# A retention layer and two MLPs on one core: the order of GpSimd's key scaling, of the weight decoding and of the last activations in the opening

## The chip, the cores and the metric

The kernel runs on one core of a Trainium2 chip. The metric is the device time of one execution in microseconds (us). A run here is one execution; the time given is the median of three.

## The reference, cut to what matters

q, k and v have 8 batches, 8 heads, 576 positions and 64 columns per head. All arithmetic is in float32. Retention is causal attention without softmax: each score is multiplied by a power of the head's decay.

```python
scores = (1 / sqrt(64)) * q @ k.T
ret = (scores * Dmat) @ v            # Dmat = gamma**(i-j) where i >= j, else 0
x = ret, heads side by side          # 4608 tokens x 512
h = x @ moe_w_in                     # 512 -> 2048
x2 = (h * sigmoid(1.702 * h)) @ moe_w_out
h2 = x2 @ moe2_w_in
out = (h2 - tanh(h2)) @ moe2_w_out   # 4608 x 512
```

## The kernel before, in words

The 4608 tokens are 36 tiles of 128 tokens; four tiles make a block of 512 tokens, and there are 9 blocks. Retention runs in chunks of 64 tokens with a carried state per head (`s_at`), so that a tile needs four groups of small products on TensorE (the PE of the profile): its scores (line 314), the carried part from the state (line 285), the scores times v (line 368, "values"), and the new state from k and v (line 338, "states"). Ahead of these the decay is put into the operands: `at_scale(t)` multiplies the keys that go into the states by a table (line 262, always on GpSimd, the profile's POOL) and the queries by another (line 263, on VectorE, the profile's DVE, for tiles 0 to 3, and on GpSimd for later tiles). The states of tile t need the keys of tile t and the first half of tile t+1.

`x_out` adds the two parts of a tile's result (lines 386, 391, 393, on DVE) and splits it into a high and a low fp32r half, `xh` (line 396, ScalarE, the profile's ACT) and `xl` (line 399, DVE). Each large product is three passes over four chunks of 128 rows (high by high, high by low, low by high), so 12 matmuls of 128x512: `mm_in` (line 527) for a first-MLP product h of one of 16 column groups f with one block, into a PSUM bank. `act_a` then runs tanh on ACT (line 540) and one DVE instruction (line 542) that reads the bank and so frees it.

The weights come as int64 words that hold float64 numbers, and are decoded on the chip. A chunk of weights takes three pieces, and `dec_piece` issues the next one, in this order per chunk: the load of a chunk ahead and `dec_b` of the chunk before (DVE line 134, ACT line 148); `dec_d` of the chunk before (DVE line 155) and `dec_a` of this one (ACT line 118, DVE line 122); `dec_a2` (DVE line 127). Chunk f, up to 15, yields `win[f]`, the operand of product f; it is complete when piece 3f+4 has run `dec_d`.

Each engine runs its instructions in the order in which the program lists them; that order is written out by hand at the end of the kernel function. The opening has these parts:

- **First visits** (`first_visit`, t = -1 to 3): the retention of tiles 0 to 3. Ahead of visit t stands `at_scale(t + 1)`; inside it, `dec_piece(pieces)` stands just ahead of `x_out`, and `follow(t)` issues the load of tile t+4 (from ACT's queue) and its scaling on GpSimd. Tile 4 takes the buffer of tile 0. Visit 3 ends with the first large product.
- **f loop** (f = 0 to 3): product f, two pieces, the activations, a visit (tiles 4 to 7), one piece, and what is left of the visit (`visit_out`: xl and the new state).
- **k loop** (k = 0 to 11): products 4+k of block 0 and the 16 products of block 1, with three pieces for each k and four from k = 8, and the visits of tiles 8 to 11 at k = 1, 4, 7 and 10. `activate(2)` leaves two products without their activation. The 32 products of the opening are numbered n = 0 to 31; even n take one of two banks `ps_h`, odd n one of two banks `acc` in turn, but for n = 31.
- **End of the opening**: the carried products of tile 12, the last two activations, and then the main loop over s from 32, whose first `mm_in` takes a bank of `ps_h`.

After that come the rest of retention, both MLPs, and the decoding and rearranging of the second MLP's weights.

Of the kernel before, what the change touches and what calls it, by code (L numbers as in the profile page):

```python
# [15 lines left out]
ALU = mybir.AluOpType  # L16

P = 128
HEADS = 8
HD = 64  # L20
# [7 lines left out]
NF = DFF // P  # L28
HP = HEADS // 2
TILES = NT // P  # L30
TPB = BLK // P
# [18 lines left out]
def kernel(  # L50
# [11 lines left out]
    nc = tc.nc  # L62
# [18 lines left out]
    qt_sb = tabs.tile([P, KD, P], F32, name="qt_sb")  # L81
    mt_sb = tabs.tile([P, 2, HP, HD], F32, name="mt_sb")
    mk_sb = tabs.tile([P, 1, HD], F32, name="mk_sb")
    jt_sb = tabs.tile([P, HEADS, 1], F32, name="jt_sb")
# [46 lines left out]
    def dec_b(m, f, c):  # L131
        _, z = half.pop((m, f, c))
        lo = stg.pop((m, f, c)).bitcast(U32).rearrange("p (n two) -> p n two", two=2)[:, :, 0]
        nc.vector.scalar_tensor_tensor(
            out=z, in0=lo, scalar=29, in1=z, op0=ALU.logical_shift_right, op1=ALU.bitwise_or
        )
        o = z.bitcast(F32)
        if (m, c) == (1, 0):
            part[m, f, c] = o
            return  # L140
        if (m, c) == (0, 0):
            s = win[f] = wts.tile([P, 2, KD, P], F32R, tag=f"wi{f}", name="wi")
            sv = s.rearrange("p a k c -> p a (k c)")
        elif m == 0 and f % 5 < 3:
            sv = wos_p.tile([P, 2, DM], F32R, tag="wos", name="ws")
        else:
            sv = st_p.tile([P, 2, DM], F32R, tag="ws", name="ws", bufs=2)
        nc.scalar.activation(out=sv[:, 0], in_=o, func=ACTF.Copy)
        half[m, f, c] = o, sv

    def dec_d(m, f, c):
        if (m, c) == (1, 0):
            return
        o, sv = half.pop((m, f, c))
        nc.vector.tensor_tensor(out=sv[:, 1], in0=o, in1=sv[:, 0].bitcast(F32), op=ALU.subtract)
        if (m, c) != (0, 0):
            part[m, f, c] = sv
        if (m, c) == (0, 1):
            wos[f] = sv

    def dec_store():
        while part:
            (m, f, c), sv = part.popitem()
            if (m, c) == (1, 0):
                w2_d[f] = dram.tile([P, BLK], F32, tag=f"w{m}{f}{c}", name="wr")
                nc.sync.dma_start(out=w2_d[f], in_=sv)
                continue
            d = dram.tile([P, 2 * DM], F32, tag=f"w{m}{f}{c}", name="wd")
            nc.sync.dma_start(out=d, in_=sv.rearrange("p a n -> p (a n)").bitcast(F32))
            wo_d[m, f] = d  # L170
# [6 lines left out]
    def dec_load(n):  # L177
        while n_load[0] < min(n, len(chunks)):
            wload(*chunks[n_load[0]])
            n_load[0] += 1  # L180

    def dec_piece(pieces=1):

        for _ in range(pieces):
            n, k = divmod(n_dec[0], 3)
            if k == 2:
                dec_store()
            if n > len(chunks):
                return
            n_dec[0] += 1  # L190
            if k == 0:
                dec_load(n + 2)
                if n:
                    dec_b(*chunks[n - 1])
                continue
            if k == 1 and n:
                dec_d(*chunks[n - 1])
            if n < len(chunks):
                (dec_a if k == 1 else dec_a2)(*chunks[n])
# [50 lines left out]
            (nc.scalar if TPB <= t < START + 2 else nc.sync).dma_start(out=a, in_=attn[t])  # L250
        at[t] = parts

    def at_scale(t):
        if t >= TILES:
            return
        for hp in (slice(0, 2), slice(2, HP)) if t == 0 else (slice(0, HP),):
            n = hp.stop - hp.start
            qv, kv = (
                at[t][i][:, 0, hp.start * P:hp.stop * P].rearrange("p (h d) -> p h d", d=d) for i, d in enumerate((P, HD))
            )  # L260
            j = jt_sb[:, 2 * hp.start:2 * hp.stop].to_broadcast([P, 2 * n, HD])
            nc.gpsimd.tensor_tensor(out=kv, in0=kv, in1=j, op=ALU.mult)
            (nc.gpsimd if t >= TPB else nc.vector).tensor_tensor(out=qv, in0=qv, in1=qt_sb[:, hp], op=ALU.mult)

    pat = ps_a.tile([P, 2, BLK], F32, name="pat")
    def halves(i):
        return slice(i * HD, (i + 1) * HD)

    def pos(t, c):
        return (2 * t + c) % CHUNKS  # L270

    def token(c):
        return slice(c * HD, (c + 1) * HD)
# [4 lines left out]
    def tile_carried(t, banks):  # L278

        parts = [c for c in (1, 0) if pos(t, c)]  # L280
        inner = [bank[:, high].rearrange("p (a c) -> p a c", a=2) for bank in banks]
        for c in parts:
            for hp in range(HP):
                for i in range(2):
                    nc.tensor.matmul(  # L285
                        inner[hp % 2][halves(i ^ hp % 2), hp // 2, token(c)], lhsT=s_at[c][halves(i), hp],
                        rhs=at[t][0][halves(i), 0, hp * P:(hp + 1) * P][:, token(c)],
                        start=True, stop=True, skip_group_check=True,
                    )
# [131 lines left out]
    def acc_pair(i):  # L421
        return [ps_acc.tile([P, BLK], F32, tag=f"acc{2 * i + b}", name="sc") for b in range(2)]

    def first_visit(t, pieces):

        banks = acc_pair(t % 2)
        last = t == TPB - 1
        if not last:
            tile_scores(t + 1, banks)
        if t < 0:  # L430
            new, parts = tile_states(t)
            scores_out(t + 1, banks)
            for _ in states_out(t, new, parts):
                pass
            return
        tile_values(t)
        new, parts = tile_states(t)
        tile_carried(t, banks)
        out = states_out(t, new, parts)
        next(out)  # L440
        if not last:
            scores_out(t + 1, banks)
        next(out)
        carried_out(t, banks)
        dec_piece(pieces)
        low_out = x_out(t)
        follow(t)
        low_out()
        if last:
            product(0)  # L450
            tile_scores(t + 1, banks)
            scores_out(t + 1, banks)

    def follow(t):
        for u in {8: (10,), 9: (11,), 10: (12,), 11: (13,)}.get(t, (t + 4,) if t < 6 else ()):
            at_load(u)
            at_scale(u)
# [3 lines left out]
    def visit_out():  # L461
        while later:
            later.pop(0)()
# [49 lines left out]

    def mm_in(s, n=None):
        j, f = divmod(s, NF)
        if n is not None and n % 2 and n < 2 * NF - 2:
            h = ps_acc.tile([P, BLK], F32, tag=f"acc{n // 2 % 2}", name="h")
        elif acc_free and s % 2 and s > PAUSE:
            h = ps_acc.tile([P, BLK], F32, tag=f"acc{acc_free.pop(0)}", name="h")
        else:  # L520
            h = ps_h.tile([P, BLK], F32, tag="h", name="h")
        hps[s] = h
        xs = (xh[j], xl[j])
        n = 0
        for k in range(KD):
            for a, b in PASS:
                nc.tensor.matmul(  # L527
                    h, lhsT=win[f][:, a, k], rhs=xs[b][:, k], start=(n == 0), stop=(n == 3 * KD - 1)
                )
                n += 1  # L530
# [36 lines left out]
    def g_store(s):  # L567
        gd[s] = dram.tile([P, BLK], F32, tag=f"g{s}", name="gd")
        nc.sync.dma_start(out=gd[s], in_=tt.pop(s))
# [277 lines left out]
    for c in range(2):  # L847
        r = halves(c)
        j = jt_sb[r].rearrange("p (h i) o -> p i h o", i=2)
        for b in range(2):  # L850
            nc.vector.tensor_tensor(
                out=mt_sb[r, b], in0=mk_sb[r].to_broadcast([HD, HP, HD]), in1=j[:, b ^ c].to_broadcast([HD, HP, HD]),
                op=ALU.mult,
# [7 lines left out]
    def product(s):  # L861
        mm_in(s, next(order))
        queue.append(s)

    def activate(keep):
        while len(queue) > keep:
            s = queue.pop(0)
            act_a(s, next(n_a))
            kept.append(s)
            if len(kept) > 2:  # L870
                g_store(kept.pop(0))

    def visit():
        attn_visit("all", False)
        follow(seen["rest"])

    for t in range(-1, TPB):
        if t + 1 < TPB:
            at_scale(t + 1)
        first_visit(t, t)  # L880

    for f in range(TPB):
        if f:
# [7 lines left out]
    for k in range(NF - TPB):  # L891
        product(TPB + k)
        activate(2)
        dec_piece()
        product(next(n_one))
        activate(2)
        dec_piece()
        if k % 3 == 0:
            product(next(n_one))
            activate(2)  # L900
        if k % 3 == 1:
            visit()
        dec_piece(2 if k > 7 else 1)
        visit_out()
    tile_carried(START, both)
    activate(0)
    carried_out(START, both)
    while kept:
        g_store(kept.pop(0))
# [17 lines left out]
    for s in range(LAG, NB * NF):  # L927
        j, f = divmod(s, NF)
# [73 lines left out]
    for u in range(pairs * QS):  # L1002
# [17 lines left out]
        n = 4 if final else 3  # L1020
# [122 lines left out]
```

## Time and profile before

| | |
|---|---|
| median of 3 runs | 1692.25 us (1690.43 to 1694.17) |
| profiled execution: its time | 1690.12 us |
| its span, first to last instruction | 1688.3 us |
| mean granted TensorE clock over the span | 0.981 |
| PE busy | 1626.7 us, 96% of the span |
| DVE busy | 1071.1 us, 63% |
| ACT busy | 866.8 us, 51% |
| POOL busy | 115.4 us, 7% |

Time lost shows as TensorE's idle time, some 62 us, and as time in which its granted clock is 0.5, which is 1.2 GHz, in place of 1.0, which is 2.4 GHz. Starts in the rows below are counted from the start of the span.

### The profile page before, as it was taken

Reading aid. Unit: us, or ns where it says so; the run is one execution under the profiler, and the core shown is the slowest. Engines: PE = TensorE matmul, PEld = TensorE weight load, DVE = VectorE, ACT = ScalarE, POOL = GpSimd, SP = SyncE. Lnnn points to the kernel's source line nnn. Section 1 sums busy time; section 2 is a strip of 40 time slices with the busy share of each in tenths; the row PEclk is TensorE's granted clock in tenths of the full one; section 3 lists DMA queues with packets and bytes.
Section 4 is the critical chain, followed back from the end, with each engine's and each line's share of the span. In section 5 each row is a group of like instructions: output and inputs, shape, how many; then the busy total and the mean of one; then the engine's idle time right before and its main releaser. Section 6 shows DMA issues by size and latency. Waiting matters only on the chain.

```text
span 1688.3 us, 29158 instructions
## 1 busy us (share of the span) xinstructions
PE 1626.7 (96%) x11082; PEld 1339.4 (79%) x11082; DVE 1071.1 (63%) x1664; ACT 866.8 (51%) x1602; POOL 115.4 (7%) x106
## 2 busy tenths in 40 slices
PE   3599899999999999999999999999999999999999
PEld 2477688888888888888888888888888888888887
DVE  2576676656666553566667786777767776667532
ACT  1344444334444443455556666666656666656532
POOL 1211111122123300000000000000000000000000
PEclk5799999999999999999999999999999999999999
DMA  6455666888889846897999889898998898989962
GB/s 195 151 178 193 205 225 226 272 293 300 294 310 345 290 163 216 285 344 272 336 348 317 288 320 341 317 338 275 326 351 316 315 318 301 310 302 320 360 214 87
DMA packets 166300, 470.96 MB, mean 279 GB/s; under 512 B 18576, under 2 KB 27792, under 8 KB 156944
## 3 DMA queue, kind: packets, MB, share of 16 engines
q1 hardware_dynamic: 153904, 439.68, 74.8%
q10 hardware_dynamic: 12256, 29.40, 4.9%
q8 instruction: 88, 1.44, 0.4%
q14 instruction: 52, 0.43, 0.1%
HBM read 349.48 MB, written 119.54 MB: 278 GB/s over the span
## 4 chain that ended last, share of the span: by engine, by line
PE 93%; DVE 2%; DMA 2%; ACT 1%; issue 1%; POOL 0%; ACTq 0%; POOLq 0%; DVEq 0%; SPq 0%
PE acc L610 24%; PE acc L612 23%; PE h L527 22%; PE x L782 10%; PE y L782 5%; PE h L769 3%; PE w L782 2%; DMA at<-in_attn_dram 1%; PE pat L338 1%; PE pat L368 1%; PE sc L285 1%; PE sc L314 1%; PE pat L285 0%; DVE z L127 0%; DVE xi L386 0%
## 5 line engine op out<-in xcount | busy, mean ns | idle before, releaser
L527 PE MATMUL h<-xh,wi 128*128 128x512 f32 x1152 | 373.1, 395 | 17.9 <-ACT xh L396 7.2
L610 PE MATMUL acc<-g,wos 128*128 128x512 f32 x1536 | 372.8, 391 | 0.0
L610 PEld LDWEIGHTS acc<-g,wos 128*128 128x128 f32 x1536 | 287.2, 188 | 60.1
L593 ACT ACTIVATE g<-gl 128x512 fp32r<-128x512 f32 x240 | 150.9, 630 | 345.5 <-PE acc L612 179.0
L612 PE MATMUL acc<-wos,g 128*128 128x512 f32 x1344 | 326.9, 390 | 0.5 <-ACT o L634 0.5
L612 PEld LDWEIGHTS acc<-wos,g 128*128 128x128 f32 x1344 | 252.3, 188 | 53.2 <-ACT o L634 1.0
L594 DVE TENSOR_TENSOR g<-gl,g 128x512 fp32r<-128x512 f32 x240 | 164.8, 688 | 188.5 <-ACT g L593 186.1
L527 PEld LDWEIGHTS h<-xh,wi 128*128 128x128 f32 x1152 | 218.1, 189 | 66.1 <-DVE t L542 7.8
L527 PE MATMUL h<-xl,wi 128*128 128x512 f32 x576 | 226.5, 393 | 0.6 <-DVE xl L399 0.6
L542 DVE SCALAR_TENSOR_TENSOR t<-t,h 128x512 f32<-128x512 f32 x144 | 98.6, 686 | 173.2 <-ACT t L540 171.6
L782 PE MATMUL x<-xo,wq 128*128 128x512 f32 x768 | 195.0, 390 | 0.0
L540 ACT ACTIVATE t<-h 128x512 f32<-128x512 f32 x144 | 84.8, 593 | 187.4 <-PE h L527 180.6
L782 PEld LDWEIGHTS x<-xo,wq 128*128 128x128 f32 x768 | 144.2, 188 | 29.9
L527 PEld LDWEIGHTS h<-xl,wi 128*128 128x128 f32 x576 | 109.2, 190 | 23.3 <-DVE xl L399 1.4
L563 DVE SCALAR_TENSOR_TENSOR pl<-pl,sq 128x512 f32<-128x512 f32 x144 | 99.6, 692 | 34.7 <-ACT pl L560 31.9
L565 DVE COPY_PREDICATED t<-marks,pl 128x512 f32<-128x512 int32 x144 | 109.6, 761 | 15.5 <-ACT g L593 0.5
L560 ACT ACTIVATE pl<-sq,abias 128x512 f32<-128x512 f32 x144 | 104.3, 724 | 4.7
L561 ACT ACTIVATE marks<-sq,sbias 128x512 f32<-128x512 f32 x144 | 102.1, 709 | 0.0
L782 PE MATMUL y<-xo,wq 128*128 128x512 f32 x384 | 97.4, 390 | 0.0
L559 DVE TENSOR_TENSOR t<-h,t 128x512 f32<-128x512 f32 x112 | 76.9, 687 | 18.1 <-ACT sq L558 9.3
L612 PE MATMUL acc<-xo,g 128*128 128x512 f32 x384 | 87.2, 390 | 0.0
L612 PEld LDWEIGHTS acc<-xo,g 128*128 128x128 f32 x384 | 72.1, 188 | 14.9
(84 smaller groups left out, 1729.0 us busy)
## 6 DMA issues: line engine op xcount, KB each, us to landing
wos<-wd SPq DMA_DIRECT2D x240, 512.0 KB, 5.1
gd<-t SPq DMA_DIRECT2D x240, 256.0 KB, 4.9
gl<-gd SPq DMA_DIRECT2D x240, 256.0 KB, 5.1
wq<-wq SPq DMA_DIRECT2D x32, 1024.0 KB, 7.5
stg<-in_w_dram SPq DMA_DIRECT2D x48, 512.0 KB, 6.3
wq<-wq SPq DMA_DIRECT2D x32, 768.0 KB, 9.2
at<-in_attn_dram SPq DMA_DIRECT2D x21, 1024.0 KB, 6.1
wd<-ws SPq DMA_DIRECT2D x32, 512.0 KB, 5.4
```

The source lines that it names most:

```text
L527: nc.tensor.matmul(h, lhsT=win[f][:, a, k], rhs=xs[b][:, k], start=(n == 0), stop=(n == 3 * KD - 1))
L540: nc.scalar.activation(out=t, in_=h, func=ACTF.Tanh, scale=0.851)
L542: nc.vector.scalar_tensor_tensor(out=t, in0=t, scalar=1.0, in1=h, op0=ALU.add, op1=ALU.mult)
L560: nc.scalar.activation(out=pl, in_=sq, func=ACTF.Square, bias=abias)
L561: nc.scalar.activation(out=small, in_=sq, func=ACTF.Relu, bias=sbias, scale=-1.0)
L563: nc.vector.scalar_tensor_tensor(out=pl, in0=pl, scalar=CB, in1=sq, op0=ALU.add, op1=ALU.mult)
L565: nc.vector.copy_predicated(out=t, mask=small.bitcast(I32), data=pl)
L593: nc.scalar.activation(out=g[:, 0], in_=t, func=ACTF.Copy)
L594: nc.vector.tensor_tensor(out=g[:, 1], in0=t, in1=g[:, 0].bitcast(F32), op=ALU.subtract)
L610: nc.tensor.matmul(acc[m], lhsT=wo[:, a, c], rhs=g[:, b], start=first, stop=last)
L612: nc.tensor.matmul(acc[m], lhsT=g[:, a, c], rhs=wo[:, b], start=first, stop=last)
L782: nc.tensor.matmul(ps, lhsT=wq[q][t][:, o // 2, o % 2 * 2 + k, a], rhs=xo[i][k][:, b], start=first and n == 0, stop=n == 5, skip_group_che ...
```

## The change

Four edits, all in the opening. The keys of tiles 0 to 3 are all put into GpSimd's queue ahead of the first visit, and so ahead of the scaling of tile 4, while the queries stay where they were. The first visits run 2, 2, 3 and 3 pieces of decoding (for t = 0 to 3) where they ran 0, 1, 2 and 3; the k loop runs three pieces for every k, so that the number at its end is the same, 58. Product n = 31 takes a bank `acc`, as the other odd ones. The last `activate(0)` stands ahead of `tile_carried(START)`.

```diff
-    def at_scale(t):
+    def at_scale(t, parts=(0, 1)):
...
-            j = jt_sb[:, 2 * hp.start:2 * hp.stop].to_broadcast([P, 2 * n, HD])
-            nc.gpsimd.tensor_tensor(out=kv, in0=kv, in1=j, op=ALU.mult)
-            (nc.gpsimd if t >= TPB else nc.vector).tensor_tensor(out=qv, in0=qv, in1=qt_sb[:, hp], op=ALU.mult)
+            if 1 in parts:
+                j = jt_sb[:, 2 * hp.start:2 * hp.stop].to_broadcast([P, 2 * n, HD])
+                nc.gpsimd.tensor_tensor(out=kv, in0=kv, in1=j, op=ALU.mult)
+            if 0 in parts:
+                (nc.gpsimd if t >= TPB else nc.vector).tensor_tensor(out=qv, in0=qv, in1=qt_sb[:, hp], op=ALU.mult)
...
-        if n is not None and n % 2 and n < 2 * NF - 2:
+        if n is not None and n % 2:
             h = ps_acc.tile([P, BLK], F32, tag=f"acc{n // 2 % 2}", name="h")
...
+    for t in range(TPB):
+        at_scale(t, (1,))
     for t in range(-1, TPB):
         if t + 1 < TPB:
-            at_scale(t + 1)
-        first_visit(t, t)
+            at_scale(t + 1, (0,))
+        first_visit(t, (0, 2, 2, 3, 3)[t + 1])
...
-        dec_piece(2 if k > 7 else 1)
+        dec_piece()
         visit_out()
+    activate(0)
     tile_carried(START, both)
-    activate(0)
     carried_out(START, both)
```

GpSimd's queue from the start of the program, before; the tiles 0, 1, 2 and 3 are at_114, at_119, at_126 and at_128, and tiles 4, 5 and 6 are at_264, at_351 and at_443 (jt_sb is the table of the keys, qt_sb that of the queries):

```order
L262 TENSOR_TENSOR at_114<-at_114,jt_sb_101 128x256 x2
L262 TENSOR_TENSOR at_119<-at_119,jt_sb_101 128x512
L262 TENSOR_TENSOR at_264<-at_264,jt_sb_101 128x512
L263 TENSOR_TENSOR at_264<-at_264,qt_sb_98 128x512
L262 TENSOR_TENSOR at_126<-at_126,jt_sb_101 128x512
L262 TENSOR_TENSOR at_351<-at_351,jt_sb_101 128x512
L263 TENSOR_TENSOR at_351<-at_351,qt_sb_98 128x512
L262 TENSOR_TENSOR at_128<-at_128,jt_sb_101 128x512
```

The same place in the changed kernel, whose lines have moved on by one to five (line 263 is now the keys, 265 the queries); tile 4 is at_270 and tile 5 at_364 there:

```order
L263 TENSOR_TENSOR at_114<-at_114,jt_sb_101 128x256 x2
L263 TENSOR_TENSOR at_119<-at_119,jt_sb_101 128x512
L263 TENSOR_TENSOR at_126<-at_126,jt_sb_101 128x512
L263 TENSOR_TENSOR at_128<-at_128,jt_sb_101 128x512
L263 TENSOR_TENSOR at_270<-at_270,jt_sb_101 128x512
L265 TENSOR_TENSOR at_270<-at_270,qt_sb_98 128x512
L263 TENSOR_TENSOR at_364<-at_364,jt_sb_101 128x512
```

The keys of tiles 2 and 3 stood behind the whole scaling of tiles 4 and 5; now nothing but the keys of tiles 0 and 1 stands ahead of them.

VectorE's queue in one step of the f loop (f = 1), before:

```order
L134 SCALAR_TENSOR_TENSOR z<-stg,z 128x512
L155 TENSOR_TENSOR wi<-z,wi 128x512
L122 TENSOR_SCALAR z<-stg 128x512
L542 SCALAR_TENSOR_TENSOR t<-t,h 128x512
L386 TENSOR_TENSOR xi<-pat,xi 128x512
L350 TENSOR_TENSOR s_at_107<-pat,s_at_107 128x256
L327 TENSOR_TENSOR p<-sc,mt_sb 128x256 x2
L127 SCALAR_TENSOR_TENSOR z<-e,z 128x512
L399 TENSOR_TENSOR xl<-xi,xh 128x4x128
L357 TENSOR_TENSOR s_at_107<-pat,s_at_106 128x256
```

And the same step now:

```order
L155 TENSOR_TENSOR wi<-z,wi 128x512
L122 TENSOR_SCALAR z<-stg 128x512
L127 SCALAR_TENSOR_TENSOR z<-e,z 128x512
L545 SCALAR_TENSOR_TENSOR t<-t,h 128x512
L389 TENSOR_TENSOR xi<-pat,xi 128x512
L353 TENSOR_TENSOR s_at_107<-pat,s_at_107 128x256
L330 TENSOR_TENSOR p<-sc,mt_sb 128x256 x2
L134 SCALAR_TENSOR_TENSOR z<-stg,z 128x512
L402 TENSOR_TENSOR xl<-xi,xh 128x4x128
L360 TENSOR_TENSOR s_at_107<-pat,s_at_106 128x256
```

The instructions are the same, and the one that starts a chunk's last third (line 134) has moved to the end of the step, so that line 155, which needs ACT's answer to it, opens the next step.

VectorE's queue at the end of the opening, from the activation of product n = 28 to that of n = 32, before:

```order
L542 SCALAR_TENSOR_TENSOR t<-t,h 128x512
L134 SCALAR_TENSOR_TENSOR z<-stg,z 128x512
L542 SCALAR_TENSOR_TENSOR t<-t,h 128x512
L155 TENSOR_TENSOR ws<-z,ws 128x512
L122 TENSOR_SCALAR z<-stg 128x512
L127 SCALAR_TENSOR_TENSOR z<-e,z 128x512
L134 SCALAR_TENSOR_TENSOR z<-stg,z 128x512
L542 SCALAR_TENSOR_TENSOR t<-t,h 128x512 x3
```

And now:

```order
L545 SCALAR_TENSOR_TENSOR t<-t,h 128x512
L155 TENSOR_TENSOR ws<-z,ws 128x512
L122 TENSOR_SCALAR z<-stg 128x512
L545 SCALAR_TENSOR_TENSOR t<-t,h 128x512
L127 SCALAR_TENSOR_TENSOR z<-e,z 128x512
L134 SCALAR_TENSOR_TENSOR z<-stg,z 128x512
L545 SCALAR_TENSOR_TENSOR t<-t,h 128x512 x3
```

One line 134 has left the stretch for the visit ahead of it, and two pieces in place of three stand between the activations of n = 29 and n = 30. The move of `activate(0)` ahead of `tile_carried(START)` changes no engine's own order, since the one is work of ACT and DVE and the other of PE.

## Rows read from the trace of the kernel before

**Rows 1.** Windows: us, each engine's busy us, granted clock, DMA share, GB/s.

```profile
10.00:60.00 50.00, 15.44 (x456) 14.17 (x456) 17.00 (x31) 9.94 (x31) 10.56 (x10) 0.50 0.48 151
66.20:94.00 27.80, 21.11 (x577) 17.12 (x577) 24.22 (x46) 14.95 (x40) 5.85 (x5) 1.00 0.58 191
181.00:200.00 19.00, 14.20 (x127) 11.02 (x125) 10.11 (x15) 7.56 (x16) 3.00 (x3) 0.91 0.72 251
200.00:1688.00 1488.00, 1483.72 (x9069) 1224.77 (x9068) 956.83 (x1465) 798.11 (x1440) 84.08 (x76) 1.00 0.83 292
```

**Rows 2.** PE's waits: total us, times, longest us.

```profile
PE pat L338 <- POOL at L262: 14.5, 3, 9.2
...
PE h L527 <- DVE t L542: 7.2, 2, 4.8
...
PE sc L285 <- DVE s_at L357: 5.6, 3, 2.4
...
PE h L527 <- DVE wi L155: 3.4, 3, 1.8
```

**Rows 3.** Timeline of POOL, 28 to 32 us: start, us, instruction, idle before.

```profile
28.41 1.04 POOL L262 TENSOR_TENSOR at<-at,jt_sb 128x512 f32<-128x512 f32 x1 [14.49 <-DMA at<-in_attn_dram]
29.41 1.26 POOL L263 TENSOR_TENSOR at<-at,qt_sb 128x512 f32<-128x512 f32 x1
30.63 1.04 POOL L262 TENSOR_TENSOR at<-at,jt_sb 128x512 f32<-128x512 f32 x1
```

**Rows 4.** Timeline of PE, 31 to 61 us: where it had waited.

```profile
31.73 1.01 PE L338 MATMUL pat<-at 64*64 64x64 f32 x26 [9.17 <-POOL at L262]
...
44.69 1.01 PE L338 MATMUL pat<-at 64*64 64x64 f32 x26 [4.20 <-POOL at L262]
...
60.45 0.80 PE L527 MATMUL h<-xh,wi 128*128 128x512 f32 x1 [7.23 <-ACT xh L396]
```

**Rows 5.** DMA issues of 5.2, 8.2 and 8.9 us: size, us to landing.

```profile
stg<-in_w_dram SPq DMA_DIRECT2D x1, 256.0 KB, 8.6
...
at<-in_attn_dram SPq DMA_DIRECT2D x1, 1024.0 KB, 9.0
...
at<-in_attn_dram SPq DMA_DIRECT2D x1, 1024.0 KB, 11.5
```

**Rows 6.** Timelines of DVE and POOL, 55 to 72 us.

```profile
55.53 0.69 DVE L155 TENSOR_TENSOR wi<-z,wi 128x512 fp32r<-128x512 f32 x1 [1.64 <-ACT wi L148]
...
57.08 1.44 POOL L263 TENSOR_TENSOR at<-at,qt_sb 128x512 f32<-128x512 f32 x1
...
57.51 1.56 DVE L127 SCALAR_TENSOR_TENSOR z<-e,z 128x512 uint32<-128x512 uint32 x1
...
71.90 0.68 DVE L127 SCALAR_TENSOR_TENSOR z<-e,z 128x512 uint32<-128x512 uint32 x1
```

**Rows 7.** Timelines of PE and DVE in the f loop.

```profile
73.57 0.69 PE L285 MATMUL sc<-at,s_at 64*64 64x64 f32 x32 [1.08 <-DVE s_at L357]
...
74.81 0.69 DVE L155 TENSOR_TENSOR wi<-z,wi 128x512 fp32r<-128x512 f32 x1 [0.70 <-ACT wi L148]
...
88.08 0.68 DVE L134 SCALAR_TENSOR_TENSOR z<-stg,z 128x512 uint32<-128x512 uint32 x1
...
94.25 0.68 DVE L134 SCALAR_TENSOR_TENSOR z<-stg,z 128x512 uint32<-128x512 uint32 x1
...
94.06 0.50 PE L527 MATMUL h<-xl,wi 128*128 128x512 f32 x1 [0.57 <-DVE xl L399]
```

**Rows 8.** Timelines of DVE and PE at the end of the opening.

```profile
182.70 1.27 DVE L155 TENSOR_TENSOR ws<-z,ws 128x512 fp32r<-128x512 f32 x1
...
186.93 0.63 ACT L148 ACTIVATE ws<-z 128x512 fp32r<-128x512 f32 x1 [4.32 <-DVE z L134]
...
188.08 1.28 DVE L542 SCALAR_TENSOR_TENSOR t<-t,h 128x512 f32<-128x512 f32 x2 [1.18 <-DMA wd<-ws]
...
188.82 0.80 PE L527 MATMUL h<-xh,wi 128*128 128x512 f32 x1 [4.80 <-DVE t L542]
```

## Prediction

> **What bounds the kernel now.** I read the windows first. From 200 us to the end PE is busy for 1483.72 of 1488 us at clock 1.00 [rows 1], so what is lost can only be won ahead of 200 us, and what is won there should come out at the end, since nothing behind waits. Between 10 and 60 us PE is busy for 15.44 of 50 us at clock 0.50, between 66 and 94 us for 21.11 of 27.8, between 181 and 200 us for 14.20 of 19 at 0.91. Then PE's waits, by who ended them [rows 2]: GpSimd's keys 14.5 us, DVE's line 542 7.2 in two waits, the state of line 357 5.6, the weights of line 155 3.4. The timelines say why. GpSimd starts on tile 4 at 28.41 after waiting 14.49 us for its load, and the keys of tile 2 come behind it at 30.63 [rows 3]; PE, which wanted them, starts at 31.73 after 9.17 us, and at the same place of the next visit at 44.69 after 4.20 us [rows 4]. Tile 2 had landed at 8.24 + 9.0 = 17.2 us and tile 3 at 8.9 + 11.5 = 20.4 us [rows 5]: the keys were late by their place in a queue, not by their data. The first large product starts at 60.45 [rows 4]. From there one PE visit follows the other at DVE's pace, until at 94.06 the second matmul of block 1's first product waits for the last xl [rows 7].
>
> **The change, part by part.** The sum is made against the profiled execution's own 1690.12 us (span 1688.30), which lies 2.1 below the median shown.
>
> *Keys first.* GpSimd needs 1.04 us for a tile's keys, so those of tiles 2 and 3 are ready by about 18.4 and 21.6 us. The states that started at 31.73 can follow at once on the products ahead of them, which ended 9.17 us earlier, at 22.6. The second wait goes too, as tile 3's keys were ready long before. That is 9.17 + 4.20 = **13.4 us** [rows 4]. What is late next is the visit's own chain, PE, DVE, ACT and DVE again: 44.69 - 31.73 - 4.20 = 8.8 us a visit. The load of tile 4 hangs on visit 0, which doesn't move, and so lands at about 28 us as before; its scaling is needed only in the f loop.
>
> *Ten pieces in the first visits.* They stand ahead of `x_out` in DVE's queue, so they are on the chain. Visits 0 and 1 get lines 122, 127 and 134, the last two at 0.68 us [rows 6, 7], line 122 for between nothing and as much: +1.6. Their weights are there: the first part of chunk 0 landed at 5.2 + 8.6 = 13.8 us [rows 5]. Visits 2 and 3 ran 15.8 us from 44.69 to 60.45. They gain one line 155 and one 134 (0.69 and 0.68, +1.4), and line 122 of visit 3 is now followed by a wait for ACT's line 118, which stands behind the visit's copies; I take +1.4 for it, an estimate, between nothing and the 1.64 us that DVE waited for ACT in that visit before [rows 6]. They lose those 1.64 us, as line 155 now comes a visit after line 134, and two delays by GpSimd like that of line 127 at 57.51, 1.56 in place of 0.68 [rows 6], which I count again below. The terms are +1.6 + 1.4 + 1.4 - 1.6 - 1.8 = +1.0; as rows that follow each other overlap a little, I take **+0.5**, between -1.5 (no wait for ACT, no cost of line 122) and +1.5.
>
> *GpSimd against DVE.* While GpSimd ran to 57.08 + 1.44 = 58.52, DVE's line 127 ended at 59.07, that is 0.55 after it, where it takes 0.68 alone [rows 6]: it had waited for GpSimd to finish. In the visits of before GpSimd mostly ran while DVE had nothing to do, because the chain was waiting for it. Now it runs beside the chain: the keys of tile 2 at 17.4 meet line 122 of visit 0, those of tile 3 at 20.5 meet the queries of tile 2 on DVE; tile 4's two instructions, from 28.4, meet xl and the queries of tile 3; tile 6's meet a line 134. That is some four meetings of 0.9 to 1.0, **+3.7 us**. Bounds: 0, if they fall into DVE's gaps, and 5.5 if six whole instructions of 1.04 or 1.26 [rows 3] are paid less one overlap. The Trainium skill, SBUF — State Buffer, section "Who interferes with whom", speaks against this change here: a DVE instruction with both inputs in SBUF and a GpSimd instruction that reads SBUF exclude each other, and whoever comes second waits for the whole of the other. The trace agrees, with the 0.55 us above. By the page alone an instruction that reads PSUM, like lines 386, 350 and 327, goes free, and the term would be the 3.7; by the rows alone those could be hit as well, which is the 5.5.
>
> So the first product starts at 60.45 - 13.4 + 0.5 + 3.7 = 51.2.
>
> *The f loop.* A step in which GpSimd doesn't run takes DVE 94.25 - 88.08 = 6.17 us, 0.70 of them the wait for ACT between lines 134 and 155 [rows 7]; the new order puts the rest of the visit and the next tanh between them, so a step takes 5.47. PE needs less: its 21.11 us of work in that stretch [rows 1] are for a little more than four steps, under 5.3 each. Without any meeting, from the first product's start to that of block 1: to the visit of f = 1 12.1 (before 73.57 - 60.45 = 13.1), two steps 10.9, and 5.1 to the last xl, 28.1 against 94.06 - 60.45 = 33.6: -5.5. The scaling of tiles 8 and 9 falls into two of the steps, before too, but now lands on both line 134 and xl; for these I add 2.4: **-3.1**, between -1.5 (both tiles paid in full, 2 x 2.3, less what was in it) and -5.5.
>
> *The k loop.* PE's three waits for line 155, 3.4 us [rows 2], came where a visit had held up DVE and the weights were a piece ahead. Four more pieces, over one product's weights, cover them: **-3.4**, between -2 and -3.4.
>
> *The end.* Before, product n = 31 waited 7.2 - 4.8 = 2.4 us for the bank of n = 28, behind a visit on DVE, and the main loop's first product waited 4.80 for that of n = 30 [rows 2, 8]. That activation was late because ACT's tanh stood behind line 148, ACT's behind DVE's line 134, and this behind three other pieces, of which GpSimd held up the first (line 155 took 1.27) [rows 8]. Then PE's clock was low: 0.91 over 19 us [rows 1] is 1.7 us of work lost. Now n = 31 takes the bank of n = 27, which is activated ahead of the visit, and the main loop's first product takes that of n = 28. That one is activated at the end of the visit, which takes DVE about 4 us (a step of 5.47 less three decoding instructions), while PE still has two products ahead of it, each about half of the 5.7 us that the first one took at half the clock (60.45 to the window at 66.2). So both waits and the slow clock go, 7.2 + 1.7 = 8.9, less 0.4 for a meeting with tile 13's scaling: **-8.5**, between -6.5 (one wait of 2.4 stays) and -8.9. The moved `activate(0)` costs nothing by itself: no engine's order changes by it. The decoding that leaves k = 8 to 11 costs nothing there, and its four pieces were paid above.
>
> Sum: -13.4 + 0.5 + 3.7 - 3.1 - 3.4 - 8.5 = **-24.2**, so 1665.9 for an execution like the profiled one; from the median shown it would be 1668.0. I predict 1666.
>
> **The rivals.**
> - *GpSimd sets the pace.* All scalings from tile 2 to tile 9, 2 x 1.04 + 6 x 2.3 = 15.9 us, fall on the chain, instead of the 3.7 + 2.4 taken: 9.8 slower than the sum, 1676. For it: an order in which DVE never waits for PE has no gaps to hide in. Against: a tile's load takes 9 to 12 us to land [rows 5], so that at most one tile is scaled in a step.
> - *The last wait stays.* If the activation of n = 30 is again late, behind pieces and GpSimd, 2.4 to 4.8 us and the low clock remain: about 1670. For it: two pieces still stand ahead of it on DVE. Against: PE has a whole product more to run.
> - *PE's clock rises early.* With the gaps of 9 us gone the first visits could run at 1.00 in place of 0.50 [rows 1]. Each has 15.44 / 4 = 3.9 us of PE work on the chain, so 3 x 1.9 and half of the first product's 5.7: 8.6 less, 1657. Against: gaps of 4 to 5 us remain in each visit.
> - *Slower: the clock stays low.* If 1.2 GHz lasted through the f loop, its 21.1 us of PE work at 1.00 [rows 1] would take 42 in place of the 28 that I give it, +14; some 10 us of the k loop's work at half the clock would use up the rest of the 24.2, and the whole k loop, 94 to 181 us, would give 1666 + 14 + 87, about 1767. It decides from 24 us lost. Against: the clock rose during the first product, and that product with its twelve matmuls stays.
> - *Won and given back.* If some transfer sets the stage behind 200 us, PE would wait there and the time stay 1690. For it: DMA is busy for 0.83 of that stretch. Against: PE has no wait in it.
>
> **How the numbers follow.** I give the sum 0.63, GpSimd 0.15, the last wait 0.10, the early clock 0.05, given back 0.04, the low clock 0.03. The best bounds together (-13.4, -1.5, 0, -5.5, -3.4, -8.9) give 1657, the worst (-13.4, 1.5, 5.5, -1.5, -2, -6.5) 1674, or 1676 from the median. The forecast, the last wait and about half of the GpSimd case make 1658 to 1677 hold some 8 in 10. About 0.2%, 3.4 us, is what a measurement of this kernel can tell from no change. Faster 0.93, same 0.04, slower 0.03.
>
> **What would show it.** Keys of tiles 2 and 3 on GpSimd at 17 and 20 us and no PE wait for them; PE's first large product near 51 us, and DVE lines 122, 134 or the xl of over 1.2 us beside GpSimd's scaling ahead of it; the first product of block 1 near 81 us; no PE wait for line 155; no wait above 1 us and clock 1.00 from there to 175 us. A first product later than 54 us would say that the chain of the visits was mis-sized; a gap of PE after 170 us, that the end was; PE waits behind 200 us, that the gain was given back.

## The result, and the profile after

The changed kernel takes 1666.2 us (median of 4, 1664.5 to 1667.2) against 1691.3 (4 runs, 1689.4 to 1694.2) of the kernel before on the same chip: ratio 0.9849, interval 0.9831 to 0.9867. The profiled execution took 1667.15 us (its span is 1665.4), 22.97 less than the 1690.12 of before; the sum of the prediction was -24.2. Lines have moved on by three from 285 on (288 is the carried part, 317 the scores, 530 a large product, 545 the release of its bank).

Windows of the kernel after, columns as in [rows 1]:

```profile
10.00:50.00 40.00, 13.54 (x448) 12.77 (x448) 21.31 (x36) 11.74 (x34) 9.10 (x7) 0.59 0.69 202
...
60.00:81.00 21.00, 15.14 (x422) 12.39 (x421) 20.63 (x36) 11.51 (x30) 5.45 (x4) 1.00 0.68 214
...
81.00:160.00 79.00, 79.00 (x783) 65.16 (x785) 51.03 (x92) 32.57 (x70) 8.29 (x6) 1.00 0.61 198
...
160.00:181.00 21.00, 20.15 (x225) 16.06 (x218) 16.47 (x27) 11.12 (x26) 5.09 (x4) 1.00 0.79 268
...
200.00:1665.00 1465.00, 1460.75 (x8867) 1205.26 (x8865) 939.59 (x1437) 788.31 (x1420) 79.43 (x72) 1.00 0.84 293
```

In the first row PE is busy for a third of the time and waits for the visits' chain in the rest; in the second DVE is busy for 20.63 of 21 us (its rows that GpSimd lengthens, below, are in this), so DVE sets the pace there; from 81 to 200 us PE has no gap but the one wait in the fourth row. PE's waits after, in total us, times and longest us, against [rows 2]:

```profile
PE sc L317 <- DVE at L265: 9.9, 3, 6.0
PE sc L317 <- issue: 6.9, 1, 6.9
PE pat L371 <- DVE xi L389: 6.5, 1, 6.5
PE sc L288 <- DVE s_at L360: 5.9, 3, 2.3
PE h L530 <- ACT xh L399: 5.1, 1, 5.1
PE pat L341 <- POOL at L263: 1.4, 2, 0.7
...
PE pat L371 <- ACT xi L302: 0.8, 1, 0.8
PE acc L615 <- ACT o L637: 0.6, 1, 0.6
```

Of the waits for keys (14.5) 1.4 us are left, and those for the bank (7.2) and for the weights of line 155 (3.4) are gone; most of what is left above is the visits' own chain. Five marks of PE, read from both timelines, say where the 22.9 us of span came from:

| mark on PE | before | after | change so far | of this part | predicted |
|---|---|---|---|---|---|
| first large product | 60.45 | 50.52 | -9.93 | -9.93 | -9.2 |
| visit of tile 8 | 104.96 | 94.60 | -10.36 | -0.43 | -3.1 (f loop) |
| visit of tile 11 | 172.91 | 158.24 | -14.67 | -4.31 | -3.4 (k loop) |
| first matmul of `acc` | 200.99 | 178.04 | -22.95 | -8.28 | -8.5 (end) |
| end of the span | 1688.3 | 1665.4 | -22.9 | 0 | 0 |

The total came out close although the f loop gave almost nothing: that miss of 2.7 us is partly covered by small ones the other way. The first mark is moreover known to some 3 us only, as e6_f_two shows below. Timeline of POOL, PE and DVE in the first visits after, against [rows 3, 4]:

```profile
19.96 1.54 POOL L263 TENSOR_TENSOR at<-at,jt_sb 128x512 f32<-128x512 f32 x1 [5.43 <-DMA at<-in_attn_dram]
...
20.52 1.53 DVE L265 TENSOR_TENSOR at<-at,qt_sb 128x512 f32<-128x512 f32 x1
...
22.15 1.13 PE L317 MATMUL sc<-at 64*64 64x64 f32 x32 [6.02 <-DVE at L265]
...
24.28 1.04 POOL L263 TENSOR_TENSOR at<-at,jt_sb 128x512 f32<-128x512 f32 x1 [2.78 <-DMA at<-in_attn_dram]
...
30.18 1.77 POOL L265 TENSOR_TENSOR at<-at,qt_sb 128x512 f32<-128x512 f32 x1
...
30.75 1.75 DVE L265 TENSOR_TENSOR at<-at,qt_sb 128x512 f32<-128x512 f32 x1
...
32.60 1.14 PE L317 MATMUL sc<-at 64*64 64x64 f32 x32 [6.93 <-issue]
...
42.55 1.13 PE L371 MATMUL pat<-p,at 64*64 64x64 f32 x32 [6.51 <-DVE xi L389]
...
50.52 0.79 PE L530 MATMUL h<-xh,wi 128*128 128x512 f32 x1 [5.14 <-ACT xh L399]
```

The keys of tiles 2 and 3 wait for nothing but their load, and PE waits for DVE's queries in their place. The rows of 1.54, 1.53, 1.77 and 1.75 us are meetings, in which DVE and GpSimd hold each other up: alone the keys take 1.04 on GpSimd, and the queries 1.26 there [rows 3] and 0.68 on DVE. Timelines of PE, DVE and POOL in the f loop after, against [rows 7]:

```profile
57.44 0.72 PE L288 MATMUL sc<-at,s_at 64*64 64x64 f32 x14 [0.55 <-DVE p L330]
...
57.63 0.91 DVE L155 TENSOR_TENSOR wi<-z,wi 128x512 fp32r<-128x512 f32 x1
...
57.95 1.72 POOL L265 TENSOR_TENSOR at<-at,qt_sb 128x512 f32<-128x512 f32 x1
...
58.46 1.49 DVE L122 TENSOR_SCALAR z<-stg 128x512 uint32<-128x512 uint32 x1
...
64.26 0.69 PE L288 MATMUL sc<-at,s_at 64*64 64x64 f32 x32 [1.68 <-DVE s_at L360]
...
67.48 0.75 DVE L330 TENSOR_TENSOR p<-sc,mt_sb 128x256 f32<-128x256 f32 x2
...
67.54 1.04 POOL L263 TENSOR_TENSOR at<-at,jt_sb 128x512 f32<-128x512 f32 x1 [7.87 <-DMA at<-in_attn_dram]
...
68.14 0.99 DVE L134 SCALAR_TENSOR_TENSOR z<-stg,z 128x512 uint32<-128x512 uint32 x1
...
68.54 1.72 POOL L265 TENSOR_TENSOR at<-at,qt_sb 128x512 f32<-128x512 f32 x1
...
69.05 1.75 DVE L402 TENSOR_TENSOR xl<-xi,xh 128x512 fp32r<-128x512 f32 x1
...
71.20 0.69 PE L288 MATMUL sc<-at,s_at 64*64 64x64 f32 x32 [1.89 <-DVE s_at L360]
```

In each step a pair of DVE rows is lengthened: 0.91 and 1.49 (0.68 and 0.42 alone), then 0.99 and 1.75 (0.68 and 0.69 alone), and in the third step 1.41 and 1.76 at 75.05 and 76.38. That is 1.30, 1.37 and 1.80 us too many. The steps of PE take 6.82, 6.94 and 7.33 (the third ends at 78.53); without the excess they are 5.52, 5.57 and 5.53. The end of the opening keeps one wait on PE:

```profile
170.43 0.69 PE L371 MATMUL pat<-p,at 64*64 64x64 f32 x32 [0.85 <-ACT xi L302]
```

### The profile page after: what moved, and what is told of

The parts are those of the page before. It is cut to its first block, busy times and chain, and to the rows that moved or that the text cites. A ratio compares the mean times of both kernels' runs of the same rounds, so it can differ in the third digit from the quotient of the medians.

```text
span 1665.4 us, 29161 instructions
## 1 busy us (share of the span) xinstructions
PE 1622.3 (97%) x11082; PEld 1336.6 (80%) x11082; DVE 1070.5 (64%) x1664; ACT 867.2 (52%) x1602; POOL 117.2 (7%) x106
## 4 chain that ended last, share of the span: by engine, by line
PE 94%; DVE 2%; DMA 2%; ACT 1%; issue 1%; SPq 0%; ACTq 0%; DVEq 0%
PE acc L613 24%; PE acc L615 23%; PE h L530 23%; PE x L785 10%; PE y L785 5%; PE h L772 3%; PE w L785 3%; PE pat L371 1%; PE pat L341 1%; DMA stg<-in_w_dram 1%; DMA at<-in_attn_dram 1%; PE sc L288 1%; PE sc L317 1%; PE pat L288 0%; DVE z L134 0%
```

## The experiments

Each kernel was run 4 times (e3_bank 10 times) beside the kernel before on the same chip; the medians of before were 1691.5 (e1 to e4), 1690.6 (e5 to e7), 1690.3 (e8 to e10) and 1692.0 (e11, e12), which is how far a median moves from one set of runs to another.

### One part alone

The edits of the change are put into the kernel before, one at a time (the moved `activate(0)` is in all of the first three); the fourth is the change without the keys.

e1_keys, the keys alone:

```diff
+    for t in range(TPB):
+        at_scale(t, (1,))
...
-            at_scale(t + 1)
+            at_scale(t + 1, (0,))
```

> Only the keys of tiles 0 to 3 stand first in GpSimd's queue; pieces, bank and last activation are as before. Theory A, the terms of the sum are separate: the 13.4 us of waits for keys go and GpSimd's meetings with DVE take back some 3, the k loop and the end keep their waits of 3.4 and 7.2 us. The first large product starts near 50 us and the time is 10 to 11 us below before, about 1681. Rival B, the parts cover for one another: without the pieces ahead the weights decide when the products can run, the first product comes no earlier than 56 us and the gain is under 5 us.

e2_pieces, the pieces alone:

```diff
-        first_visit(t, t)
+        first_visit(t, (0, 2, 2, 3, 3)[t + 1])
...
-        dec_piece(2 if k > 7 else 1)
+        dec_piece()
```

> Only the decoding pieces are moved: 2, 2, 3, 3 in the first visits, three for every k. Theory A: the first visits change by less than 1.5 us, since PE waits for keys there anyway, the three waits for line 155 in the k loop go (3.4 us and about 1 us of restarts), and the end keeps most of its waits, as n = 31 still takes the bank of n = 28: 4 to 7 us below before, about 1686. Rival B: the f loop gains the 0.7 us of each step, 3 more, and the end loses its waits too, since they came from the pieces of the last steps: 12 us below, about 1679.

e3_bank, the bank of n = 31 alone:

```diff
-        if n is not None and n % 2 and n < 2 * NF - 2:
+        if n is not None and n % 2:
```

> Only product n = 31 takes the other bank, and the last activations stand ahead of tile 12's carried products, which changes no engine's order. Theory A: the two waits at the end, 2.4 and 4.8 us, go, but the copy of tile 12's carried part still stands behind the late activations on ACT, so that PE waits for it some 2 us ahead of tile 12's values: 5 to 7 us below before, about 1685. Rival B: the late activations are what counts, whatever bank is taken, and the wait only moves to tile 12's values: less than 2 us.

e4_no_keys, the changed kernel with the keys where they were before:

```diff
-    for t in range(TPB):
-        at_scale(t, (1,))
...
-            at_scale(t + 1, (0,))
+            at_scale(t + 1)
```

> The change without the keys: pieces, bank and last activations as in the changed kernel, the keys as before. Theory A: the k loop's 4.4 us and the end's 8.3 us are won, the opening up to the first product stays within 1.5 us: 12 to 13 us below before, about 1679, and with the keys alone the two make the whole change of 23 to 25 us. Rival B: the parts cover for one another, and it is less than 8 us below.

Measured: 1675.1 (0.9903, 0.9885 to 0.9921), 1682.9 (0.9950, 0.9935 to 0.9965), 1688.8 (0.9987, 0.9977 to 0.9996) and 1680.2 (0.9933, 0.9918 to 0.9949), so -16.3, -8.6, -2.7 and -11.2; the whole change is -25.1. The keys are the largest part, and larger than expected; the pieces gave more than the 4 to 7 us of theory A, the bank lies between its two theories, and e4_no_keys stays somewhat under theory A. The marks of PE, read as in the table above, say where each kernel gains against before:

| kernel | first large product | f loop | k loop | end |
|---|---|---|---|---|
| e1_keys | -14.34 | -0.95 | +0.52 | -0.16 |
| e2_pieces | +1.90 | +0.82 | -4.31 | -5.57 |
| e3_bank | -0.38 | -0.86 | -0.09 | -1.70 |
| e4_no_keys | +2.35 | -0.34 | -4.32 | -8.28 |
| the whole change | -9.93 | -0.43 | -4.31 | -8.28 |

So the k loop's 4.3 us come from the pieces alone, and the end's 8.3 need pieces and bank. The bank alone is worth little, because the wait moves on instead of ending; PE's timeline of e3_bank at the end of the opening:

```profile
187.80 1.13 PE L371 MATMUL pat<-p,at 64*64 64x64 f32 x32 [4.89 <-ACT xi L302]
```

The values of tile 12 now wait 4.89 us for ScalarE's copy of the carried part, which stands behind the last pieces and activations; with the pieces moved too, this wait is the 0.85 us shown above. Keys and the rest add up to -27.5, 2.4 more than the whole gains. The intervals of the three kernels are each some 3 us wide to either side, so this is not clear of noise; a reading that would fit it, that the pieces cost less beside PE's waits for keys than on a chain without them, is not shown. PE's timelines of e1_keys and e2_pieces at the first large product,

```profile
46.11 0.79 PE L530 MATMUL h<-xh,wi 128*128 128x512 f32 x1 [7.23 <-ACT xh L399]
```

```profile
62.35 0.80 PE L530 MATMUL h<-xh,wi 128*128 128x512 f32 x1 [5.14 <-ACT xh L399]
```

are 14.3 us earlier and 1.9 us later than the 60.45 of before [rows 4].

### What the f loop pays for

e5_no_scaling leaves out GpSimd's scaling of tiles 4 to 9, so part of the computation is missing:

```diff
-        if t >= TILES:
+        if t >= TILES or TPB <= t < 10:
```

> The changed kernel without GpSimd's scaling of tiles 4 to 9, keys and queries, so that the output of those tiles lacks the decay's tables; everything else stays. Theory A, GpSimd holds up DVE and that took back what the f loop should have won: DVE's lines 265, 122 and 155 of the first visits lose the 2.6 us that they wait there, and lines 122, 134 and 402 of the f loop some 4.4, a step falls from 6.9 and 7.3 us to 5.5, the time to 7 us below the changed kernel, about 1659. Rival B, the step is set by the round trip over PE and ACT: it stays at 6.5 us or more, and the time falls by less than 4 us.

e6_f_two takes one piece out of each step of the f loop and puts it into the k loop:

```diff
-        dec_piece(2)
+        dec_piece()
         activate(0)
...
-        dec_piece()
+        dec_piece(2 if k < TPB else 1)
```

> The changed kernel with two pieces in place of three in each step of the f loop, and four in place of three for k = 0 to 3, so that the number is again 58. Theory A, the f loop runs at DVE's pace: four pieces, about 0.73 us each, leave it, and the k loop, where PE is the bound, takes them at no cost: 2.5 to 3.5 us below the changed kernel, about 1663. Rival B: GpSimd's instructions then meet other DVE instructions, or the weights are late again in the k loop (a wait for line 155), and the time stays within 1.5 us.

Without the scaling: 1660.2 us, 6.0 less than the changed kernel. By the marks the f loop gives 4.05 of this; the first large product, at 48.04, is 2.48 earlier. PE's timeline of e5_no_scaling in the f loop:

```profile
54.02 0.72 PE L288 MATMUL sc<-at,s_at 64*64 64x64 f32 x14 [0.55 <-DVE p L330]
...
59.55 0.69 PE L288 MATMUL sc<-at,s_at 64*64 64x64 f32 x32 [0.40 <-DVE s_at L360]
...
65.10 0.69 PE L288 MATMUL sc<-at,s_at 64*64 64x64 f32 x32 [0.51 <-DVE s_at L360]
...
66.55 0.51 PE L317 MATMUL sc<-at 64*64 64x64 f32 x19 [0.53 <-issue]
...
71.46 0.69 PE L288 MATMUL sc<-at,s_at 64*64 64x64 f32 x32 [0.45 <-DVE s_at L360]
```

The first two steps take 5.53 and 5.55 us: what the steps of the changed kernel come to when the excess of the lengthened DVE rows is taken off. In these the meetings with GpSimd are the whole of the difference. The third takes 6.36; no DVE row is lengthened in it, but PE stops for 0.53 us within its scores (the row at 66.55), for a reason that the profile doesn't show, and DVE then waits for PE. Fewer pieces did nothing: 1665.8 us (0.9848, 0.9833 to 0.9863). Theory A of e6_f_two falls. Its first visits are those of the changed kernel, instruction for instruction, and yet its first large product starts at 47.60, 2.9 us earlier than in the profile above: the keys of tiles 2 and 3 start at 17.21 and 20.12 there, and not at 19.96 and 24.28, as the loads landed earlier. So a mark in the first visits is known to some 3 us from one execution.

### Where the pieces stand

e7_ahead puts the ten pieces ahead of each visit, behind its queries; DVE then decodes while PE runs the visit's first products:

```diff
-        first_visit(t, (0, 2, 2, 3, 3)[t + 1])
+        dec_piece((0, 2, 2, 3, 3)[t + 1])
+        first_visit(t, 0)
```

> The changed kernel with the ten pieces of the first visits put ahead of each visit, behind the queries on DVE, in place of just ahead of x_out. Theory A, the pieces stand on the visits' chain: DVE waits 3.4 to 4.5 us for PE at the new place, so that 1 to 3 us of decoding in each of visits 1 to 3 lie beside it, and the first product comes 3 to 5 us earlier, near 46 us; 3 to 5 us below the changed kernel. Rival B: PE's first product waits for something else by then (tile 3's load or keys at 24 to 25 us, or the weights), and less than 1.5 us is won.

e8_queries adds to it, in `first_visit`, the queries of the tile after the next one ahead of the low part (and takes them out of the loop for tiles 2 and 3); e9_ahead_f_two is e7 with the f loop of e6, e10_queries_f_two e8 with the f loop of e6:

```diff
         low_out = x_out(t)
+        if t + 2 < TPB:
+            at_scale(t + 2, (0,))
         follow(t)
```

> The kernel with the ten pieces ahead of their visits (1659.4 us, first large product at 44.4), and besides the queries of tiles 2 and 3 scaled one visit earlier, in the 0.69 us in which VectorE waits for the activation of the rounded part, ahead of the low part. TensorE still waits there 5.08 us at 20.81 and 4.57 us at 29.07 for a chain that ends with the scaling of the queries on VectorE. Theory A (these 0.69 us, with the row's wait behind the low part, are on the chain): two visits gain 0.7 to 1.2 us each, first large product 1.4 to 2.4 us earlier from the same landings, median about 1657.5. Theory B (another step, the scores' mask or the carried products, comes last once the queries are there, or the landing of tile 2 near 18 to 20 us holds the queue up): within 0.7 us of 1659.4.

> The kernel with the ten pieces ahead of their visits (1659.4 us), and besides two pieces in a step of the f loop in place of three, and four in a step of the k loop where k is under 4. Theory A (with the first visits out of the way the pieces of the f loop are on its chain, three collisions of 0.5 to 1 us each): f loop shorter by 1.5 to 3 us, median 1656.5 to 1658. Theory B (as in the changed kernel, GpSimd's scaling alone lengthens the steps, whatever pieces stand beside it): within 0.8 us of 1659.4.

> Both edits of the two other kernels of this call at once. If each is worth what theory A gives it, about 1655; if neither is on the chain, within 1 us of 1659.4. If the f loop's start moves with the queries but its length doesn't, the gain of the one at the first large product is found again at the end, whatever the other does.

e7_ahead takes 1659.4 us (0.9814, 0.9799 to 0.9829), 6.8 less than the changed kernel and more than expected. Its first large product starts at 44.39: 6.1 us before that of the changed kernel's profile, 3.2 before that of e6_f_two, so the place of the pieces, ahead of `x_out`, was on the chain. The f loop gives 2.2 us besides (the visit of tile 8 is at 86.32, against 94.60): of its three steps only the one from 56.46 to 63.16 is lengthened, as GpSimd's scaling fell otherwise. The mark lies even before that of the keys alone (46.11), where visits 1 to 3 keep one, two and three pieces on the chain; the 1.7 us between them are within the spread. The other three take 1659.1, 1658.8 and 1659.4: theory A fails in all. In e8_queries the third visit did start earlier (27.64 against 29.07), but DVE's and ACT's timelines show what came next:

```profile
28.85 0.42 DVE L122 TENSOR_SCALAR z<-stg 128x512 uint32<-128x512 uint32 x1
...
31.36 0.34 ACTq L250 DMA_DIRECT2D at<-in_attn_dram  x1
...
31.82 0.67 ACT L118 ACTIVATE e<-stg 128x512 f32<-128x512 f32 x1 [4.22 <-DMA at<-in_attn_dram]
...
32.52 1.80 DVE L127 SCALAR_TENSOR_TENSOR z<-e,z 128x512 uint32<-128x512 uint32 x1 [3.25 <-ACT e L118]
```

DVE waits 3.25 us for ACT's line 118, with the visit behind it in its queue, and line 118 starts right behind the issue of tile 5's load, which stands ahead of it in ACT's queue. The words were not what it waited for: line 122 reads the same words, and DVE ran it at 28.85 without a wait, 2.97 us before line 118. The issue itself starts 0.1 us after tile 4's load has landed (19.57 + 11.7); whether it waits for that, no run shows.

### Who issues the loads

The same one-line edit in two kernels, the changed one (e11_sync_loads) and e8_queries (e12_queries_sync): the loads of tiles 4 to 13 go into SyncE's queue.

```diff
-            (nc.scalar if TPB <= t < START + 2 else nc.sync).dma_start(out=a, in_=attn[t])
+            nc.sync.dma_start(out=a, in_=attn[t])
```

> The changed kernel (1666.2 us) with the loads of tiles 4 to 13 issued by SyncE's queue alone in place of ScalarE's. Theory A (a load that ScalarE issues waits in its queue for an earlier transfer, and the activations behind it wait with it, on the chain of the visits): the rows of line 356, which start 6.1 and 6.3 us after the row ahead of them, come earlier, first large product 2 to 4 us earlier, median 1662 to 1664. Theory B (line 356 starts within 0.1 to 0.6 us of the end of VectorE's line 353, so it waits for VectorE and TensorE, and the issue ahead of it lies in that wait): within 1 us of 1666.2.

> The kernel with the pieces ahead and the queries one visit earlier (1659.1 us), with the same loads on SyncE's queue alone. There ScalarE's line 118 starts 0.46 us after the issue of tile 5's load, in all three profiles of such kernels (30.84 after 30.39, 31.82 after 31.36, 30.36 after 29.90), and VectorE waits for it 1.64 to 3.25 us with the whole visit behind it. Theory A (the issue holds line 118 up): that row comes 1.5 to 3 us earlier and the first large product with it, median 1656 to 1657.5. Theory B (the words that line 118 reads land only then, and the issue just stands beside): within 1 us of 1659.1.

e11_sync_loads takes 1661.6 us (0.9815, 0.9799 to 0.9831), 4.6 less than the changed kernel; e12_queries_sync takes **1654.9 us** (1654.1 to 1658.0; ratio 0.9782, 0.9767 to 0.9797), 4.2 less than e8_queries and the fastest of all. The size of theory A came out in e11, nearly, but not its route. Line 356 starts at 24.33 and 34.44 there, each time right behind DVE's line 353 (23.81 and 33.92), as theory B read the rows, and the first large product, at 47.05, is about within the spread of the changed kernel (47.60 to 50.52). What is clear of that spread is won in the f loop, 4.4 us by the marks. Timelines of PE, DVE and POOL of e11_sync_loads there:

```profile
58.92 0.69 PE L288 MATMUL sc<-at,s_at 64*64 64x64 f32 x32 [0.36 <-DVE s_at L360]
...
60.71 1.04 POOL L263 TENSOR_TENSOR at<-at,jt_sb 128x512 f32<-128x512 f32 x1 [10.86 <-DMA at<-in_attn_dram]
...
61.20 0.69 DVE L389 TENSOR_TENSOR xi<-pat,xi 128x512 f32<-128x512 f32 x1
...
61.71 1.30 POOL L265 TENSOR_TENSOR at<-at,qt_sb 128x512 f32<-128x512 f32 x1
...
61.81 0.41 DVE L353 TENSOR_TENSOR s_at<-pat,s_at 128x256 f32<-128x256 f32 x1
...
62.14 0.74 DVE L330 TENSOR_TENSOR p<-sc,mt_sb 128x256 f32<-128x256 f32 x2
...
62.80 0.75 DVE L134 SCALAR_TENSOR_TENSOR z<-stg,z 128x512 uint32<-128x512 uint32 x1
...
63.48 0.68 DVE L402 TENSOR_TENSOR xl<-xi,xh 128x512 fp32r<-128x512 f32 x1
...
64.55 0.69 PE L288 MATMUL sc<-at,s_at 64*64 64x64 f32 x32 [0.58 <-DVE s_at L360]
```

GpSimd's two instructions, as many as before, now lie beside lines 389, 353 and 330, whose first operand is in PSUM (`pat`, `sc`), and none of these is longer than without GpSimd. The step takes 5.63 us and the next one 5.55. Tile 7 was scaled at 47.30, beside the first large product. So the earlier landing moved the scaling to where it meets nothing: from the first large product to the fourth visit 23.05 us, against 28.01 in the changed kernel. Part of the gain is lost again at the end of the opening, 2.6 us in e11_sync_loads (0.8 in e12_queries_sync against e8_queries). PE's timeline of e11_sync_loads there:

```profile
163.60 0.84 PE L371 MATMUL pat<-p,at 64*64 64x64 f32 x32 [1.91 <-ACT xi L302]
```

GpSimd scales tile 13 at 158.14 in that kernel, beside two pieces on DVE (lines 127 and 134, 1.50 and 1.67 us), where in the changed kernel it met one (line 134, 1.42, tile 13 at 166.60), and so the wait of 0.85 us has become 1.91. In e12_queries_sync line 118 runs at 25.55, directly behind `xh` at 25.01, and the first large product starts at 40.87, 4.55 us earlier than in e8_queries: with the issue out of ACT's queue nothing holds line 118 up, as theory A said. The f loop gives 2.4 us besides.

## Why the prediction was right, point by point

**Keys first, -13.4: right.** Alone they moved the first large product by 14.3 us, and no meeting took any of it back: the lengthened DVE rows ahead of it are as long together as before, 1.73 us. The starts foretold, 17 and 20 us, were 19.96 and 24.28 in the profiled execution, because the loads took longer there, and 17.21 and 20.12 in that of e6_f_two.

**Pieces +0.5 and GpSimd +3.7: right in one execution, in part by luck, and the place of the pieces was not weighed.** Ahead of the product four DVE rows (20.52, 30.75, 37.83 and 38.89) are lengthened, by 0.85, 1.07, 0.45 and 1.06, 3.4 us. Two of the places foretold are among them, the queries of tiles 2 and 3; the others are lines 155 and 122 beside tile 5. In the execution of e6_f_two, whose first visits are the same, only two rows are (lines 122 and 127 at 35.31 and 36.68), by 1.73 us together. With the pieces the mark is 4.4 us behind that of the keys alone in the one execution (50.52 against 46.11), 1.5 in the other (47.60). So the 4.2 foretold for both terms hung on when the loads landed. That the pieces could stand where they cost nothing, and that those of visits 1 to 3 had cost something before, the prediction left out: e7_ahead shows 3.2 to 6.1 us at the first large product.

**The f loop, -3.1: the step that failed.** The free step of 5.47 us was right (5.53 and 5.55 without scaling), and so nearly was the whole without meetings, 28.1 us to the second matmul of block 1's first product: in e5_no_scaling 29.15 (48.04 to 77.19), in e11_sync_loads 28.79 (47.05 to 75.84). "For these I add 2.4" was too little: tiles 8 and 9 cost 1.37 + 1.80 = 3.2, and tile 7 another 1.30. Tile 7's scaling had lain beside the first large product before (POOL 64.80); with that product 9.9 us earlier and the load not as much, it fell into a step. So 4.5 in place of 2.4, and the free part is 1.0 longer; of these 3.1 us the marks show 2.7 (-3.1 to -0.43), and block 1's first product came near 83.4, not 81. Here a rule of the Trainium skill, SBUF — State Buffer, section "Who interferes with whom" (a DVE instruction with two SBUF inputs contends with a GpSimd instruction that reads SBUF; one with at most one such input does not, outside the modes in which DVE uses both of its port pairs), is borne out on both sides: `xl` 1.75 in place of 0.69 in the changed kernel, line 330, with one operand in PSUM, an unchanged 0.74 in e11_sync_loads. Line 122 reads one operand from SBUF and is lengthened too, 1.49 in place of 0.42; whether it runs in such a mode, no row shows. How many meetings there are hangs on when a load lands.

**The k loop, -3.4: mis-sized, -4.31.** No wait for line 155 is left. From the visit of tile 8 to that of tile 11 each of the three waits (0.60, 1.00, 1.8) gave about 0.3 us more than its length; what these are was not tried.

**The end, -8.5: right, -8.28.** The two waits and the slow clock are gone, and bank and pieces are both needed: alone they give 1.70 and 5.57.

**The rivals.** GpSimd setting the pace was the right mechanism at the wrong size: the scaling of tiles 4 to 9, 13.8 of its 15.9 us, is worth 6.0. The last wait did not stay. The low clock did not come, 1.00 from 60 us on, and nothing was given back, as PE has one wait of 0.6 us behind 200 us. The early clock came about in single executions and was worth nothing: one run of the changed kernel with a mean clock of 0.999 took 1667.0 us, the others (0.986 to 0.988) 1664.5 to 1667.2. The last section shows an execution of that kind.

## What to carry to other kernels

When a queue is put right, look next at what stands on the new chain: here the place of ten pieces of decoding was worth 3 to 6 us once the waits for keys were gone, and only moving them showed it. Price a contention by the excess of the lengthened rows; if the excess taken off the steps gives the step without the rival engine, the account is closed, and then ask what sets the moment of the meeting. Look at the loads that an engine on the chain issues: its queue dates the transfer, and with it the work that the transfer sets off on a third engine, and the issue can hold up what stands behind it. Taking them out of ACT's queue was worth 4.6 and 4.2 us here, although part of it came back as a meeting at another place; so follow the moved work to its end.

## What the runs showed of the hardware that was not expected

The granted clock of a stretch did not tell how long its rows take. The profile of e4_no_keys shows 1.00 from 10 us on; windows and PE's timeline of that kernel:

```profile
10.00:62.00 52.00, 14.91 (x448) 13.67 (x448) 17.76 (x35) 11.51 (x33) 7.56 (x7) 1.00 0.50 156
```

```profile
62.80 0.79 PE L530 MATMUL h<-xh,wi 128*128 128x512 f32 x1 [5.14 <-ACT xh L399]
```

The first matmul takes 0.79 us, as at a granted 0.5 (0.80, [rows 4]), and PE's work ahead of it is as much as in [rows 1], 14.91 us against 15.44; once PE has run the first large product, such a row takes 0.50 in the same execution. So in this execution a row's own length, and not the clock column, says at what speed the engine ran.
